# Attention scores of five batches over 64 rows, two heads side by side, in two bursts a batch

## The chip, the cores and the metric

The kernel runs on one core of one Trainium2 chip. The metric is the device time of one execution in microseconds (us); the span of an execution runs from its first to its last instruction and is a little shorter. The engines are called as in the profile: PE (TensorE, matmuls), PEld (its weight loads), ACT (ScalarE), DVE (VectorE), POOL (GpSimd) and SP (the queue that issues most DMAs). A matmul multiplies a stationary operand, loaded by LDWEIGHTS, with a moving operand that is streamed past it column by column; the result goes to a PSUM bank, of which there are eight.

## The reference

```python
def _attn_ref(q, k, v):                       # 8 batches, 8 heads, 576 positions, head size 64
    scores = np.matmul(q, k.transpose(0, 1, 3, 2)) / np.sqrt(64)
    rel = pos[:, None] - pos[None, :]
    mask_plain = (rel >= 0) & (rel < 32)                       # heads 0 to 3
    mask_dil = (rel >= 0) & (rel < 32 * 4) & (rel % 4 == 0)    # heads 4 to 7
    ... masked softmax over the keys, then attn @ v

def _moe_ref(x, w_tok1, w_tok2, w_ch1, w_ch2):   # x: 576 positions x 512 channels of a batch
    h = np.maximum(xt @ w_tok1, 0.0) @ w_tok2    # mixes tokens, 576 -> 256 -> 576
    u = x + h.transpose(0, 2, 1)
    h2 = np.maximum(u @ w_ch1, 0.0) @ w_ch2      # mixes channels, 512 -> 1536 -> 512
    return u + h2
```

The attention's output, heads side by side, is the `x` of the second part.

## The kernel before

The eight batches go through a software pipeline whose order is written out by hand. `gen_main(b)` is the main loop of batch b: the two channel matmuls, first `gp` (with its relus into `gt`, on ACT and DVE), then `yp` (evicted by DVE into `o`, stored by SP). It yields after every few matmuls an estimate of its own time, and `interleave` inserts the other batches' steps at given places on that clock: values, token mixing (`h1p`, `up`) of batch b+1 and casts, transposes and scores of batch b+2. So during main loops 1 to 5 the scores of batches 3 to 7 are computed. Odd batches' main loops also hold the 64-position tails of two batches (`gt` tiles of PSUM, `yp` first).

**Scores.** Heads go in pairs hp = 0..3; the first 64 partitions hold one head of the pair, the other 64 the second. `kt` holds k transposed in natural order, `kr` in order of remainder by 4. `qz[hp][:, h]` is q of head h with the other head's 64 rows set to zero, so one matmul over all 128 rows gives the scores of head h. Plain heads (hp 0, 1) need, for each head, blocks of 128 keys by 160 queries in a bank `sc`, and a small bank `sm` for the last block and the tail. Dilated heads (hp 2, 3) need four blocks of 128 by 128, one for each remainder, and a small bank. The exponential (ACT) goes to `attp` or `attd`; POOL multiplies by the band mask. Batches 0 to 2 hide scores in another way, with an added matmul of the identity and `veil`, or (batch 2) as the later ones.

**From batch 3 on** (`by_dma`), q and k are transposed by DMA into `qta` (`qt` in the profile), `kra` (`kr`) and `tta` (`tt`, the tails). `place_steps` then copies them: POOL writes `kt` and `qz` of the plain heads and the tails, DVE `qz` of the dilated heads and the last 128 keys of `kt`. `score_steps` gives the twelve places of a batch's score pieces; between two of them 6 or 12 matmuls of `yp` stand on PE.

**Banks.** `main` has three banks in turn (`gp`, `yp`), `sc` two (scores only, `sc` and `sm`), `fl` three (values `av`, `h1p`, `up`, transposes).

Of the kernel before, what the change touches and what calls it, by code (L numbers as in the profile page):

```python
# [16 lines left out]
S = 576  # L17
D = 64
WINDOW = 32
# [14 lines left out]
PTL = 4 * PST  # L34
PW = PTL + 192
DTL = 512
DW = DTL + 320
# [20 lines left out]
def _np_dtail():  # L58
    p = np.arange(128)[:, None]
    j = np.arange(64)[None, :]  # L60
    reach = WINDOW * DILATION
    out = []
    for k0 in (384, 512):
        rel = (512 + j) - (k0 + p)
        out.append((rel >= 0) & (rel < reach) & (rel % DILATION == 0))
    return np.stack(out, axis=1).astype(np.float16)
# [3 lines left out]
def kernel(  # L70
# [40 lines left out]
    def mult(eng, out, a, b):  # L111
# [4 lines left out]
    CW = 2 * 128 + BLK + 128  # L116
# [4 lines left out]
    dtail = const[:, 256 + BLK:CW].rearrange("p (x y c) -> p x y c", x=1, y=2)  # L121

    veil = fixed("veil", [128, BLK + 128])
# [4 lines left out]
         _np_dtail().reshape(128, 128)], axis=1)  # L128
# [29 lines left out]
    def emit_fixed():  # L158
# [5 lines left out]
        for a in attp:  # L164
            nc.gpsimd.memset(
                a[:, :, 0:PTL].rearrange("p h (b c) -> p h b c", c=PST)[:, :, :, BLK:PST], 0.0)
            nc.gpsimd.memset(a[:, :, PTL:PW], 1.0)
        for a in attd:
            nc.vector.memset(a[:, :, DTL:DW], 1.0)

# [190 lines left out]
    def place_steps(b):  # L361

        halves = [slice(0, 64), slice(64, 128)]

        def tails():
            eng = nc.vector if b == 3 else nc.gpsimd
            for h in range(2):
                eng.tensor_copy(out=qza[halves[h], :, h, 512:S], in_=tta[halves[h], :, 0:64])
            eng.tensor_copy(out=kta[:, :, 512:S], in_=tta[:, :, 64:128])

        def plain(hp):
            nc.gpsimd.tensor_copy(out=natural(kt[hp][:, 0:512]), in_=kra[:, hp].rearrange("p r m -> p m r"))
            for h in range(2):
                nc.gpsimd.tensor_copy(out=natural(qz[hp][halves[h], h, 0:512]),  # L374
                                      in_=qta[halves[h], hp].rearrange("p r m -> p m r"))

        def dil(h):
            nc.vector.tensor_copy(out=qza[halves[h], 2:4, h, 0:512],
                                  in_=qta[halves[h], 2:4].rearrange("p a r m -> p a (r m)"))

        def dil_k():
            for hp in (2, 3):
                nc.vector.tensor_copy(out=natural(kt[hp][:, 384:512]),
                                      in_=kra[:, hp, :, 96:128].rearrange("p r m -> p m r"))

        return ([tails] + [lambda hp=hp: plain(hp) for hp in range(2)],
                [lambda h=h: dil(h) for h in range(2)] + [dil_k])
# [27 lines left out]

    def scores_plain(b, hp):
        a = attp[hp]
        blocks = a[:, :, 0:PTL].rearrange("p h (b c) -> p h b c", c=PST)
        tl = a[:, :, PTL + 64:PTL + 128]
        veils = veiled(b, hp)  # L420
        wide, narrow = (veil[:, 0:BLK], veil[:, 0:64]) if veils else (None, None)
        for h in range(2):
            p = bank("sc", 2, f"sc_{b}_{hp}_{h}")
            for kb in range(3):
                score(b, hp, h, p[:, BLK * kb:BLK * kb + BLK], slice(128 * kb, 128 * kb + 128),
                      slice(128 * kb, 128 * kb + BLK), wide)
# [5 lines left out]
        for h in range(2):  # L432
            score(b, hp, h, p[:, BLK * h:BLK * h + BLK], slice(384, 512), slice(384, 384 + BLK), wide)
        for h in range(2):
            score(b, hp, h, p[:, 320 + 64 * h:384 + 64 * h], slice(512, 640), slice(512, S), narrow)
        nc.scalar.activation(  # L436
            out=blocks[:, :, 3, 0:BLK], in_=p[:, 0:320].rearrange("p (h c) -> p h c", c=BLK),
            func=AF.Exp, scale=0.125)
        nc.scalar.activation(
            out=tl, in_=p[:, 320:448].rearrange("p (h c) -> p h c", c=64), func=AF.Exp, scale=0.125)  # L440
        if not veils:
            mult(nc.gpsimd, blocks[:, :, :, 0:BLK], blocks[:, :, :, 0:BLK], band)
            mult(nc.gpsimd, tl, tl, band[:, 0, :, 0:64])
        yield 0.21

    def scores_dil(b, hp):
        a = attd[hp - 2]
        diag = a[:, :, 0:DTL].rearrange("p h (r c) -> p h r c", c=128)
        tl = a[:, :, DTL + 64:DTL + 320].rearrange("p h (x c) -> p h x c", c=128)[:, :, :, 0:64]
        veils = veiled(b, hp)  # L450
        for h in range(2):
            p = bank("sc", 2, f"sc_{b}_{hp}_{h}")
            for r in range(4):
                score(b, hp, h, p[:, 128 * r:128 * r + 128], kra[:, hp, r] if by_dma(b) else slice(r, 512, 4),
# [4 lines left out]
        for h in range(2):  # L459
            for x in range(2):  # L460
                score(b, hp, h, p[:, 128 * h + 64 * x:128 * h + 64 * x + 64],
                      slice(384 + 128 * x, 512 + 128 * x), slice(512, S),
                      veil[:, BLK + 64 * x:BLK + 64 * x + 64] if veils else None)
        nc.scalar.activation(
            out=tl, in_=p[:, 0:256].rearrange("p (h x c) -> p h x c", x=2, c=64),
            func=AF.Exp, scale=0.125)
        if not veils:
            mult(nc.gpsimd, diag, diag, band[:, :, :, 0:128])
            mult(nc.gpsimd, tl, tl, dtail)
        yield 0.12  # L470

    def values(b, h):
# [4 lines left out]
        if hp < 2:  # L477
# [7 lines left out]
            c0 = 3 * PST + (64 if odd else 128)  # L485
            c1 = PTL + (0 if odd else 64)
            nc.tensor.matmul(out=av[:, 4], lhsT=a[:, c0:c0 + 128], rhs=va[:, 3, h, :],
# [454 lines left out]
```

## Time and profile before

| | |
|---|---|
| median of 3 runs | 297.87 us (297.7 to 298.11) |
| the profiled execution | 297.69 us, span 295.8 us, granted clock 1.000 |
| PE | busy 280.8 us, 95% of the span |
| PEld | busy 218.7 us, 74% |
| POOL | busy 186.2 us, 63% |
| DVE | busy 156.9 us, 53% |
| ACT | busy 136.6 us, 46% |

A matmul's listed duration includes the way through the array, and consecutive matmuls overlap, so what a group of them costs PE is read from the distance between starts in the timeline, not from the durations. Main loop 1 starts at about 69.6 us of the span, loop 2 at 108.4, loop 3 at 138.1, loop 4 at 173.3, loop 5 at 203.1 and loop 6 at 238.

### The profile page before, as it was taken

The page shows a single profiled execution, that of the slowest core. Times are in us where ns is not written, and L with a number is a line of the kernel's source. Part 1 is how long each engine was busy: PE and PEld are TensorE (multiplying, and loading weights), DVE is VectorE, ACT ScalarE, POOL GpSimd, SP SyncE. Part 2 cuts the span into 40 slices and gives each one's busy share as a digit, 9 for nine tenths or more (in the row PEclk, how much of TensorE's full clock was granted, in tenths as well). Part 3 has the DMA queues.
Part 4 walks back from the last instruction along what each step waited for, and adds up shares of the span by engine and source line. Part 5 has one row for each costly group of instructions (what it writes and reads, how often), then busy time and mean ns, then how long its engine had stood idle before and what let it go on. Part 6 is the DMA issues. An engine that isn't in the chain of part 4 may idle for free.

```text
span 295.8 us, 7055 instructions
## 1 busy us (share of the span) xinstructions
PE 280.8 (95%) x2810; PEld 218.7 (74%) x2810; DVE 156.9 (53%) x303; ACT 136.6 (46%) x266; POOL 186.2 (63%) x256
## 2 busy tenths in 40 slices
PE   5698999988999999999999999999999999999994
PEld 2586589976776986698776976797777976896593
DVE  5766347855828637466743555486654364422022
ACT  3763336356663634556346715474355625224500
POOL 6982045538999899959976999679985920000000
PEclk9999999999999999999999999999999999999999
DMA  7999999999958978179987978399965220531032
GB/s 214 264 202 160 207 320 209 289 265 277 242 112 216 289 228 168 31 175 324 229 149 166 323 219 179 59 216 317 196 127 107 73 74 0 82 115 38 0 89 92
DMA packets 103473, 52.09 MB, mean 176 GB/s; under 512 B 71792, under 2 KB 102384, under 8 KB 103440
## 3 DMA queue, kind: packets, MB, share of 16 engines
q1 hardware_dynamic: 99200, 46.55, 63.8%
q0 software_dynamic: 2640, 3.91, 7.5%
q10 hardware_dynamic: 1600, 1.18, 1.3%
q8 instruction: 22, 0.36, 0.5%
q14 instruction: 11, 0.09, 0.1%
HBM read 37.04 MB, written 9.44 MB: 157 GB/s over the span
## 4 chain that ended last, share of the span: by engine, by line
PE 78%; DMA 10%; POOL 6%; issue 3%; ACT 2%; SPq 0%; DVE 0%; POOLq 0%; ACTq 0%
PE gp L646 26%; PE yp L665 25%; PE h1p L513 4%; PE up L525 4%; DMA w<-in_moe_w_ch_dram 4%; PE yp L685 4%; PE sc L407 3%; PE gt L637 3%; DMA l_k<-in_k_dram 2%; DMA l_vn<-in_v_dram 2%; DMA l_q<-in_q_dram 2%; POOL vv L103 1%; PE sm L407 1%; PE h1p L511 1%; PE av L483 1%
## 5 line engine op out<-in xcount | busy, mean ns | idle before, releaser
L665 PE MATMUL yp<-w,gt 128*128 128x256 f16 x756 | 92.2, 273 | 0.0
L107 ACT ACTIVATE gt<-gp 128x512 f16<-128x512 f32 x76 | 45.4, 597 | 78.5 <-PE gp L646 78.2
L665 PEld LDWEIGHTS <-gt 128*128 128x128 f16 x768 | 76.8, 106 | 5.2 <-issue 0.3
L646 PEld LDWEIGHTS <-w 128*128 128x128 f16 x384 | 40.0, 114 | 24.4 <-issue 2.0
L113 POOL TENSOR_TENSOR attp<-attp,const 128x1280 f16<-128x1280 f16 (+1 forms) x24 | 36.9, 1564 | 18.1 <-ACT attp L436 18.0
L646 PE MATMUL gp<-utd,w 128*128 128x512 f16 x120 | 45.6, 380 | 0.0
L646 PE MATMUL gp<-utm,w 128*128 128x512 f16 x120 | 45.5, 379 | 0.0
L675 DVE TENSOR_TENSOR o<-yp,u 128x512 f32<-128x512 f32 x31 | 21.2, 688 | 45.1 <-PE yp L665 42.5
L646 PE MATMUL gp<-uT,w 128*128 128x512 f16 x144 | 36.2, 379 | 1.5 <-DMA w<-in_moe_w_ch_dram 0.8
L113 POOL TENSOR_TENSOR attd<-attd,const 128x1024 f16<-128x1024 f16 (+1 forms) x24 | 32.8, 1398 | 0.0
L113 DVE TENSOR_TENSOR xn<-av,rec 128x320 f16<-128x320 f32 x64 | 31.5, 492 | 2.2
L407 PEld LDWEIGHTS <-kt 128*128 128x128 f16 x272 | 22.2, 101 | 5.1 <-issue 1.5
L427 ACT ACTIVATE attp<-sc 128x480 f16<-128x480 f32 x32 | 17.8, 572 | 9.8 <-PE sc L407 9.2
L531 DVE TENSOR_TENSOR u<-up,xn 128x512 f16<-128x512 f32 x26 | 18.0, 691 | 8.1 <-PE up L525 8.1
L374 POOL COPY qz<-qt 64x512 f16<-64x512 f16 x20 | 21.6, 1081 | 0.6
L103 POOL CAST c_q<-l_q 128x512 f16<-128x512 f32 x31 | 18.9, 615 | 4.4 <-DMA l_q<-in_q_dram 4.4
L109 DVE TENSOR_SCALAR gt<-gp 128x512 f16<-128x512 f32 x20 | 13.8, 688 | 12.4 <-PE gp L646 11.9
L103 POOL CAST c_k<-l_k 128x512 f16<-128x512 f32 x29 | 17.7, 613 | 2.8 <-DMA l_k<-in_k_dram 2.6
L456 ACT ACTIVATE attd<-sc 128x512 f16<-128x512 f32 x32 | 17.9, 600 | 2.7 <-PE sc L407 2.5
L407 PE MATMUL sc<-qz,kt 128*128 128x160 f16 (+1 forms) x144 | 18.1, 228 | 1.0 <-DVE kt L315 1.0
L107 ACT ACTIVATE h<-h1p 128x256 f16<-128x256 f32 x29 | 11.1, 383 | 16.5 <-PE h1p L513 16.4
L502 DVE RECIPROCAL rec<-av 128x5 f32<-128x5 f32 x64 | 12.1, 189 | 11.2 <-PE av L499 5.9
(139 smaller groups left out, 487.8 us busy)
## 6 DMA issues: line engine op xcount, KB each, us to landing
out_dram<-o SPq DMA_DIRECT2D x72, 128.0 KB, 3.0
l_q<-in_q_dram SPq DMA_DIRECT2D x15, 512.0 KB, 6.6
l_k<-in_k_dram SPq DMA_DIRECT2D x14, 512.0 KB, 7.0
l_vn<-in_v_dram SPq DMA_DIRECT2D x32, 128.0 KB, 5.6
l_vd<-in_v_dram SPq DMA_DIRECT2D x16, 256.0 KB, 3.8
w<-in_moe_w_ch_dram POOLq DMA_DIRECT2D x6, 512.0 KB, 8.6
lt<-in_q_dram SPq DMA_DIRECT2D x8, 128.0 KB, 4.0
l_vt<-in_v_dram SPq DMA_DIRECT2D x8, 128.0 KB, 3.7
```

What stands on the lines that cost most here:

```text
L103: eng.tensor_copy(out=out, in_=in_)
L107: nc.scalar.activation(out=out, in_=in_, func=AF.Relu)
L109: eng.tensor_scalar_max(out=out, in0=in_, scalar1=0.0)
L113: eng.tensor_tensor(out=out, in0=x, in1=y, op=ALU.mult)
L374: nc.gpsimd.tensor_copy(out=natural(qz[hp][halves[h], h, 0:512]), in_=qta[halves[h], hp].rearrange("p r m -> p m r"))
L407: nc.tensor.matmul(out=out, lhsT=lhsT, rhs=qz[hp][:, h, queries], start=hide is None, stop=True)
L427: nc.scalar.activation(out=blocks[:, h, 0:3, 0:BLK], in_=p[:, 0:3 * BLK].rearrange("p (b c) -> p b c", c=BLK), func=AF.Exp, scale=0.125)
L456: nc.scalar.activation(out=a[:, h, 0:DTL], in_=p, func=AF.Exp, scale=0.125)
L531: nc.vector.tensor_tensor(out=u16(b, s), in0=blocks4(p), in1=blocks4(xn[b][:, s]), op=ALU.add)
L646: nc.tensor.matmul(out=p, lhsT=w3_block(cb, mb), rhs=uT[(b, cb)][0], start=(i == 0), stop=(i == 3))
L665: nc.tensor.matmul(out=p[:, c], lhsT=gta[:, mb, a0:m0 + 512:4] if half else gta[:, mb, a0:a0 + 128], rhs=w4[mb][:, c], start=(mb == 0), st ...
L675: nc.vector.tensor_tensor(out=blocks4(o32), in0=blocks4(p), in1=u16(b, s), op=ALU.add)
```

## The change

For batches 3 to 7 the scores are computed by `scores_twin`, a burst for the plain heads (g = 0) and one for the dilated heads (g = 1). Each matmul takes the 64 rows of its own head: keys from the head's half of `kt` or `kr`, queries straight from `qt` and `tt`. The two heads of a pair alternate and write to different banks. A burst is 24 matmuls in a row and takes six banks: both of `sc`, all three of `fl`, one of `main`. Before, a batch's scores were 44 matmuls of 128 rows in twelve pieces; now they are 48 of 64 rows in two. Queries of the plain heads come out in the order of the remainder by 4, and the exponential reads PSUM with a stride so that it writes in order. The copies into `qz` are gone for these batches; the copies of the last keys move from DVE to POOL. The tails' weights go to a buffer of their own, `attt`, also for batches 0 to 2, whose small bank now holds 128 columns and two tail blocks of 64 for a head (before 160 and one). The first burst is placed behind the relus of `gp`.

On PE, in main loop 2 (scores of batch 4; `sc_0_0` is the bank of the first head of the pair 0, `sc_0_1` that of the second). Before, where the first piece stands between matmuls of `yp`:

```order
L665 MATMUL yp_0_2213<-w_85,gt 128x256
L407 LDWEIGHTS kt
L407 MATMUL sc_0_0_2228<-qz,kt 128x160
L407 LDWEIGHTS kt
L407 MATMUL sc_0_0_2228<-qz,kt 128x160
L407 LDWEIGHTS kt
L407 MATMUL sc_0_0_2228<-qz,kt 128x160
L665 LDWEIGHTS gt
L665 MATMUL yp_0_2213<-w_85,gt 128x256
```

After, the first rows of the burst in the same place:

```order
L736 MATMUL yp_0_2220<-w_85,gt 128x256
L476 LDWEIGHTS kt
L476 MATMUL sc_0_0_2228<-qt,kt 128x160
L476 LDWEIGHTS kt
L476 MATMUL sc_0_1_2229<-qt,kt 128x160
L476 LDWEIGHTS kt
L476 MATMUL sc_0_0_2228<-qt,kt 128x160
L476 LDWEIGHTS kt
L476 MATMUL sc_0_1_2229<-qt,kt 128x160
```

Three matmuls of one head became the first of 24 in which the heads alternate; behind the burst 30 matmuls of `yp` follow (26 in odd loops) before the second burst.

On ACT, in the same main loop (the exponentials, and the copies `utd` that the next main loop's `gp` reads). Before:

```order
L427 ACTIVATE attp_74<-sc_1_1_2294 128x3x160
L436 ACTIVATE attp_74<-sm_1_2316 128x2x160
L439 ACTIVATE attp_74<-sm_1_2316 128x2x64
L583 COPY utd<-utm_88 128x512
L456 ACTIVATE attd_75<-sc_2_0_2326 128x512
L456 ACTIVATE attd_75<-sc_2_1_2345 128x512
L464 ACTIVATE attd_75<-sm_2_2364 128x2x2x64
L583 COPY utd<-utm_88 128x512
L456 ACTIVATE attd_76<-sc_3_0_2374 128x512
```

After:

```order
L500 ACTIVATE attp<-sc_0_5_2233 128x2x128
L500 ACTIVATE attt<-sc_0_5_2233 128x2x2x64
L500 ACTIVATE attd_74<-sc_1_0_2314 128x512
L500 ACTIVATE attd_74<-sc_1_1_2315 128x512
L500 ACTIVATE attd_75<-sc_1_2_2316 128x512
L500 ACTIVATE attd_75<-sc_1_3_2317 128x512
L500 ACTIVATE attt<-sc_1_4_2318 128x2x2x64
L500 ACTIVATE attt<-sc_1_5_2319 128x2x2x64
L649 COPY utd<-utm_88 128x512 x2
```

The two copies `utd` stood among the dilated heads' exponentials; now both stand behind them.

On POOL, between the casts of batch 4 and its masks. Before:

```order
L368 COPY qz<-tt 64x4x64 x2
L369 COPY kt<-tt 128x4x64
L372 COPY kt<-kr 128x512
L374 COPY qz<-qt 64x512 x2
L372 COPY kt<-kr 128x512
L374 COPY qz<-qt 64x512 x2
L113 TENSOR_TENSOR attp_73<-attp_73,const 128x2x4x160
```

After:

```order
L367 COPY kt<-kr 128x512
L364 COPY kt<-tt 128x4x64
L367 COPY kt<-kr 128x512
L370 COPY kt<-kr 128x128 x2
L112 TENSOR_TENSOR attp<-attp,const 128x8x160
```

Six copies into `qz` left POOL, and two short ones of `kt` came from DVE.

```diff
-    attp = [fixed(f"attp{i}", [128, 2, PW]) for i in range(2)]
-    attd = [fixed(f"attd{i}", [128, 2, DW]) for i in range(2)]
+    attpa = fixed("attp", [128, 2, 2, PW])
+    attp = [attpa[:, i] for i in range(2)]
+    attd = [fixed(f"attd{i}", [128, 2, DTL]) for i in range(2)]
+    attt = fixed("attt", [128, 4, 2, TW])
...
-        for a in attd:
-            nc.vector.memset(a[:, :, DTL:DW], 1.0)
+        nc.vector.memset(attt, 1.0)
...
         def tails():
-            eng = nc.vector if b == 3 else nc.gpsimd
-            for h in range(2):
-                eng.tensor_copy(out=qza[halves[h], :, h, 512:S], in_=tta[halves[h], :, 0:64])
-            eng.tensor_copy(out=kta[:, :, 512:S], in_=tta[:, :, 64:128])
+            nc.gpsimd.tensor_copy(out=kta[:, :, 512:S], in_=tta[:, :, 64:128])
...
-    def scores_plain(b, hp):
...
+    def tail_scores(b, hp, p, c0):
+        for h in range(2):
+            for x in range(2):
+                c = c0 + 128 * h + 64 * x
+                v0 = BLK + 128 * (hp // 2) + 64 * x
+                score(b, hp, h, p[:, c:c + 64], slice(384 + 128 * x, 512 + 128 * x), slice(512, S),
+                      veil[:, v0:v0 + 64] if veiled(b, hp) else None)
...
+    def scores_twin(b, g):
+
+        tags = (("sc", 2), ("sc", 2), ("fl", 3), ("fl", 3), ("fl", 3), ("main", 3))
+        ps = [bank(*tags[i], f"sc_{b}_{g}_{i}") for i in range(6)]
+        small = ps[4:6]
+
+        def twin(hp, banks, c, keys, queries):
+            for h in range(2):
+                rows = slice(64 * h, 64 * h + 64)
+                n = c.stop - c.start
+                nc.tensor.matmul(out=banks[h][:, c], lhsT=keys(rows), rhs=queries(rows), start=True, stop=True)
+
+        for j in range(2):
+            hp = 2 * g + j
+            if g == 0:
+                for kb in range(3):
+                    twin(hp, ps[2 * j:2 * j + 2], slice(BLK * kb, BLK * kb + BLK),
+                         lambda rows: kt[hp][rows, 128 * kb:128 * kb + 128],
+                         lambda rows: qta[rows, hp, :, 32 * kb:32 * kb + 40])
+            else:
+                for r in range(4):
+                    twin(hp, ps[2 * j:2 * j + 2], slice(128 * r, 128 * r + 128),
+                         lambda rows: kra[rows, hp, r], lambda rows: qta[rows, hp, r])
+        for j in range(2):
+            hp = 2 * g + j
+            if g == 0:
+                twin(hp, small, slice(256 + 128 * j, 384 + 128 * j),
+                     lambda rows: kt[hp][rows, 384:512], lambda rows: qta[rows, hp, :, 96:128])
+            for x in range(2):
+                twin(hp, small, slice(128 * j + 64 * x, 128 * j + 64 * x + 64),
+                     lambda rows: kt[hp][rows, 384 + 128 * x:512 + 128 * x], lambda rows: tta[rows, hp, 0:64])
+        yield 0.87
+
+        def main(hp):
+            for h in range(2):
+                p = ps[2 * (hp % 2) + h]
+                if g == 0:
+                    exp(plain_blocks(hp)[:, h, 0:3, 0:BLK].rearrange("p b (m r) -> p b m r", r=4),
+                        p[:, 0:3 * BLK].rearrange("p (b r m) -> p b m r", r=4, m=40))
+                else:
+                    exp(attd[hp - 2][:, h], p)
...
     def score_steps(b, t0, dt, offs=(0.0, 0.7, 2.0), places=None):
 
         steps = []
+        if by_dma(b):
+            for g in range(2):
+                for i, f in enumerate([scores_twin(b, g)] * 2):
+                    steps.append((t0 + g * dt, 0.86 * (i == 0), lambda f=f: next(f)))
+            return steps
...
-            steps += score_steps(3, 22.2, 2.8) + at(9.0, 0.6, cast_steps(3))
+            steps += score_steps(3, 25.2, 4.2) + at(9.0, 0.6, cast_steps(3))
...
-                steps += at(2.0, 0.6, cast_steps(b + 2)) + score_steps(b + 2, 15.0 + late, 2.6)
-                steps += at(8.5, 0.7, dma_steps(b + 2)) + at(13.0, 0.4, place_steps(b + 2)[0])
+                steps += at(2.0, 0.6, cast_steps(b + 2)) + score_steps(b + 2, 16.6 + 1.25 * late, 4.5)
+                steps += at(8.5, 0.7, dma_steps(b + 2)) + at(12.0, 0.4, place_steps(b + 2))
```

More of the change, by code (lines that the diff above doesn't have):

```diff
@@ L33 @@
 PST = 256
-PTL = 4 * PST
-PW = PTL + 192
+PW = 4 * PST
 DTL = 512
-DW = DTL + 320
+TW = 320
 CBS = (2, 0, 3, 1)
@@ L458, in scores_dil @@
         p = small_bank(b, hp)
[L459 to L466, printed above, removed]
+        tail_scores(b, hp, p, 0)
```

129 lines of the change are left out of this document (74 added, 55 removed).

## The prediction

> **What bounds the kernel now.** I read the page's engine shares first, then the chain that ended last, then busy time by stretch, the list of PE's waits, and last the timeline around the scores.
>
> ```profile
> PE 280.8 (95%) x2810; PEld 218.7 (74%) x2810; DVE 156.9 (53%) x303; ACT 136.6 (46%) x266; POOL 186.2 (63%) x256
> PE 78%; DMA 10%; POOL 6%; issue 3%; ACT 2%; SPq 0%; DVE 0%; POOLq 0%; ACTq 0%
> 108.38:238.00 129.62, 128.74 (x1263) 100.20 (x1262) 72.97 (x128) 64.81 (x124) 111.65 (x138) 1.00 0.76 179
> 238.00:291.60 53.60, 53.60 (x451) 40.25 (x449) 18.68 (x36) 16.70 (x28) 0.48 (x1) 1.00 0.23 60
> PE sc L407 <- ACT attd L456: 0.3, 2, 0.2
> ```
>
> In the stretches the columns after the length are busy PE, PEld, DVE, ACT, POOL, then clock, DMA share and GB/s. From main loop 2 on PE lacks 0.9 us of 129.6, and nothing of the last 53.6; POOL is at 86% there but PE hardly waits for it. So a microsecond less in PE's stream is a microsecond less in the end, if PE then finds no new wait. The clock is full. What a score piece costs PE is the distance from its start to the next row's:
>
> ```profile
> 95.29 0.39 PE L550 MATMUL tpu<-const,u 128*128 128x128 f16 x4
> 95.51 0.37 PE L407 MATMUL sc<-qz,kt 128*128 128x160 f16 x3
> 95.72 0.82 PE L665 MATMUL yp<-w,gt 128*128 128x256 f16 x6
> 96.38 0.37 PE L407 MATMUL sc<-qz,kt 128*128 128x160 f16 x3
> 97.24 0.36 PE L407 MATMUL sm<-qz,kt 128*128 128x160 f16 x4
> 97.44 0.82 PE L665 MATMUL yp<-w,gt 128*128 128x256 f16 x6
> 103.12 0.28 PE L407 MATMUL sm<-qz,kt 128*128 128x64 f16 x4
> 103.23 0.82 PE L665 MATMUL yp<-w,gt 128*128 128x256 f16 x6
> 103.89 0.39 PE L407 MATMUL sc<-qz,kr 128*128 128x128 f16 x4
> 104.11 0.82 PE L665 MATMUL yp<-w,gt 128*128 128x256 f16 x6
> ```
>
> Three matmuls of 160 columns take 0.21 us (0.070 each), four of 128 take 0.22 (0.055), four of 64 take 0.11 (0.0275), the plain small bank 0.20, six of `yp` 0.66 (0.11): time goes by columns, and zero rows cost as much as others.
>
> **The change, part by part.** Removed from PE: four plain pieces and two small banks, 4 x 0.21 + 2 x 0.20 = 1.24 us, and four dilated pieces and two small banks, 4 x 0.22 + 2 x 0.11 = 1.10. That is 2.34 us a batch, 11.7 us for five.
>
> Added: burst 1 has 6 pairs of 160 columns, 2 of 128 and 4 of 64; burst 2 has 8 of 128 and 4 of 64. No row of before shows two half-height matmuls together, so I bound a pair. Low end: its heads stream side by side, and a pair costs what one full matmul of its columns does: 6 x 0.070 + 2 x 0.055 + 4 x 0.0275 = 0.64, and 8 x 0.055 + 4 x 0.0275 = 0.55, together 1.19 us. High end: one after the other, 2.38 us. The heads use different partitions, weights and banks, so nothing that the rows show is shared but the order of issue. I take the low end, with the 64-column pairs put at up to 0.055, since 0.0275 for one is the shortest distance in these rows and may be an issue limit: 1.19 to 1.41, taken as 1.30. Saved: 5 x (2.34 - 1.30) = 5.2 us; the ends are 5.75 saved and 0.2 lost.
>
> The edges. Each burst goes from full height to half height and back: 2 bursts x 2 x 5 batches = 20 edges. What an edge may cost is read from one matmul's own times:
>
> ```profile
> L407 PE MATMUL sc<-qz,kt x144: 217/232/245, 8.0 to 227.1; 128*128 128x160 f16 x96, 128*128 128x128 f16 x48
> L407 PEld LDWEIGHTS <-kt x272: 95/98/117, 8.0 to 233.7; 128*128 128x128 f16 x136
> ```
>
> A 160-column matmul lasts 232 ns from start to end and holds the next back for 70: 162 ns are its way out. A weight load lasts 98 ns and is hidden now, for starts are closer than that. If PE must be empty at an edge, the edge costs 0.16 us; if the load can't run ahead either, 0.26; if neither, 0. The nearest row for 0 is the change of kind from transposes to scores at 95.51, which costs nothing (0.22 for four, as within scores), but it does not change the array's division. I take the way out alone, 0.16, because loads are hidden everywhere in these rows: 20 x 0.16 = 3.2 us, ends 0 and 5.2. The Trainium skill bears on this: "TensorEngine Tiling (Array Packing)", section Tiling Modes, states that a change of the tiling mode, not of the tile alone, drains the TensorE. No run here shows it yet; by the row of 95.51 the sum below would be 292.5, by that rule it stays at 295.7.
>
> A stall that goes. In even loops the dilated exponentials stood behind a copy `utd`:
>
> ```profile
> 133.86 0.28 PE L407 MATMUL sm<-qz,kt 128*128 128x64 f16 x4
> 134.29 0.38 PE L407 MATMUL sc<-qz,kr 128*128 128x128 f16 x4 [0.15 <-ACT attd L456]
> 132.16 1.09 ACT L583 COPY utd<-utm 128x512 f16<-128x512 f16 x1
> 133.14 1.10 ACT L456 ACTIVATE attd<-sc 128x512 f16<-128x512 f32 x2
> ```
>
> 0.11 us after 133.86 the array is free, the next piece starts at 134.29: 0.32 us lost, in two loops by PE's waits (x2): 0.64 us gained. Late next there are the copies themselves, now both behind burst 2's exponentials. Two exponentials take 1.10, so 0.55 each. Burst 2 starts 0.69 + 30 x 0.11 + 0.32 (two edges) = 4.3 us after burst 1; its first bank is readable some 0.4 us later, four exponentials take 2.2, two small ones 0.8, and the two copies of 1.09 end at 9.9; the next main loop starts at 0.69 + 0.61 + 90 x 0.11 + 0.64 = 11.8. Covered by 1.9 us.
>
> Banks between the bursts. Burst 2 reuses burst 1's banks, so ACT must have read them.
>
> ```profile
> L427 ACT ACTIVATE attp<-sc 128x480 f16<-128x480 f32 x32 | 17.8, 572 | 9.8 <-PE sc L407 9.2 <-POOL qz L374 0.5
> L464 ACT ACTIVATE attd<-sm 128x256 f16<-128x256 f32 x16 | 6.1, 384 | 3.2 <-PE sm L407 3.2
> L583 ACT COPY utd<-utm 128x512 f16<-128x512 f16 x10 | 10.8, 1086 | 4.1 <-DMA utm<-u 4.1
> L101 ACT COPY uT<-tpu 128x512 f16<-128x512 f16 x3 | 1.8, 585 | 2.9 <-PE tpu L559 2.9
> L101 ACT CAST w1n<-w_p 128x512 f16<-128x512 f32 x2 | 1.2, 585 | 1.6 <-PE w_p L783 1.6
> ```
>
> The plain exponentials now read with a stride of 40 fp32 values. `uT` on ACT reads PSUM in that way (all of ACT's `uT` are the reordered ones) and lasts 585 ns, the straight cast `w1n` also 585; `utd`, strided from SBUF, 1086. A strided read of PSUM is nearest to `uT`, so I keep 572. Then the eight exponentials of burst 1 (four at 0.55, four at 0.384) end 0.4 + 2.2 + 1.5 = 4.1 us after its start, and burst 2 needs their last bank at 4.3 + 0.44: no wait. The high end, 1086, is a rival.
>
> New waits for `fl`. In main loop 1 burst 1 stands directly behind the last transposes, which use `fl`:
>
> ```profile
> 95.49 0.58 ACT L101 COPY uT<-tpu 128x512 f16<-128x512 f16 x1 [1.59 <-PE tpu L559]
> 96.38 0.41 DVE L103 COPY uT<-tpu 128x512 f16<-128x512 f16 x1
> ```
>
> PE wants the bank at 95.51 + 0.21 = 95.72 and gets it at 96.07: 0.35 us, once. The last of them, read by DVE until 96.79, would make it 0.9 at most, but DVE loses the `qz` and `kt` copies ahead of it. In later loops `fl` was left long before.
>
> Small bank of batches 1 and 2: 2 x 0.055 + 4 x 0.0275 = 0.22 for 0.195, for two pairs, and twice that in batch 1 with its `veil` matmuls: 0.15 us. Batch 0's 0.1 us and the start-up lie under PE's waits there:
>
> ```profile
> 10.61 0.40 PE L393 MATMUL tp_t<-const,c_t 128*128 128x128 f16 x4 [1.24 <-POOL c_t L103]
> 29.19 10.31 PE L646 MATMUL gp<-uT,w 128*128 128x512 f16 x47 [0.80 <-DMA w<-in_moe_w_ch_dram]
> 3.60 1.27 DVE L169 MEMSET attd<- 128x640 f16 x2
> L374 POOL COPY qz<-qt 64x512 f16<-64x512 f16 x20 | 21.6, 1081 | 0.6
> L383 DVE COPY kt<-kr 128x128 f16<-128x128 f16 x10 | 13.6, 1404 | 0.1
> 126.26 0.37 PE L407 MATMUL sc<-qz,kt 128*128 128x160 f16 x3
> 123.78 2.21 POOL L374 COPY qz<-qt 64x512 f16<-64x512 f16 x2
> 129.02 6.26 POOL L113 TENSOR_TENSOR attp<-attp,const 128x1280 f16<-128x1280 f16 x4 [3.04 <-ACT attp L436]
> ```
>
> The new memset has twice the elements of the two at 3.60, so DVE is 1.3 us later there, and the constants' DMA is a quarter larger; PE's 1.24 us of waiting for POOL at 10.61 cover it. I set 0; the ends are 0 and 0.3.
>
> POOL loses 4 x 1.08 us a batch, DVE the 1.4 us copies, which move to POOL two a batch. Both count 0: POOL already waited 3.04 us for ACT before the masks, and PE for neither. In loop 2 the last copy ended at 123.78 + 2.21 = 126.0; without four of 1.08 it is 121.7, for a burst that stands one `yp` group (0.66) ahead of 126.26. SP issues the same transposes in the same order.
>
> **Sum** against the profiled execution: 297.69 - 5.2 + 3.2 - 0.64 + 0.35 + 0.15 = 295.55. It stood 0.18 below the median of the runs, so the median would be 295.7, or 2.1 us (0.7%) less.
>
> **The rivals.**
> - Dear edges: the load after an edge is not hidden either, 0.26 each. For it: nothing can be loaded ahead into an array that is to be divided anew. Against: all loads in the rows run ahead. 295.7 + 2.0 = 297.7, no change.
> - Cheap edges, 0.03 each: 295.7 - 2.6 = 293.1. For it, the gapless change at 95.51.
> - The change doesn't do what it says: the heads of a pair run one after the other. The bursts cost 2.38 us instead of 1.30, so 295.7 + 5 x 1.08 = 301.1, slower. It decides from 1.7 us a batch for the two bursts on, where the edges eat what is saved. For it, that PE takes its matmuls in order and no row shows two at once; against, that the heads share no rows, weights or bank.
> - Loads not hidden at half height: each head waits for its own load and columns, so a pair costs 98 + 70 = 168, 153 or 126 ns: 6 x 0.168 + 2 x 0.153 + 4 x 0.126 + 8 x 0.153 + 4 x 0.126 = 3.55 us a batch, and 295.7 + 5 x 2.25 = 306.9. The Trainium skill's "TensorE: Matmul & The Clock Gate", section Part 3, says that a load overlaps matmuls in flight only where its row group differs, and here every second load has the same. The rows of now contradict it at full height: 98 ns loads stand under starts 70 ns apart, all on the same rows. So its chance is small.
> - Strided exponentials as slow as `utd`: 0.4 + 4 x 1.09 + 2 x 0.73 + 2 x 0.384 = 7.0 us against 4.74, so PE waits 2.25 us in each batch for the last bank: 295.7 + 11.2 = 306.9.
>
> **How the numbers follow.** Chances: my forecast 0.47 (its own range 294.2 to 297.2, by edges of 0.09 to 0.23), dear edges 0.22, cheap edges 0.12, one after the other 0.11, loads not hidden 0.04, slow exponentials 0.04. Ends of the range: cheap edges without any limit for the 64-column pairs (0.5 less) at the low side, 292.6; dear edges with the whole 0.9 us of the bank wait and 0.3 at the start at the high side, 298.6. The last three cases, 0.19, stay out. The least that a measurement of this kernel can tell from no change is about 0.2%, 0.6 us. Faster: 0.42 of my case, 0.12 of the cheap edges and 0.03 of the dear ones, 0.57. Same: 0.04 and 0.12, 0.16. Slower: 0.01, 0.07, and the last three, 0.27.
>
> **What would show it.** In the timeline of after: pairs of `sc` matmuls starting together, or 0.070 us apart for both; the distance from the last `yp` before a burst to the burst's first matmul, less 0.11, is an edge, likewise behind it. The whole burst 1, from that `yp` to the next, should take about 1.0 us, burst 2 0.9. ACT's plain exponentials should stay at 570 to 600 ns. PE's waits should hold no row of bursts against ACT, but for one of about 0.35 us near 95.7. The `utd` copies should end before `gp`. I would be wrong if bursts take 1.4 us or more each, or if the next `gp` or `av` waits for ACT or POOL.

## The result and the profile after

The changed kernel takes 294.38 us (median of 5 runs, 293.95 to 295.36); the kernel before, run beside it, 297.87 us (296.65 to 298.11). The ratio is 0.9896, 95% interval 0.9869 to 0.9923: 3.5 us or 1.0% faster. The profiled execution took 293.95 us with a span of 292.2 us, against 297.69 and 295.8.

The engine shares, the chain that ended last by engine, and the stretch from main loop 2 to about main loop 6 of the changed kernel (columns as in the prediction):

```profile
PE 278.1 (95%) x2850; PEld 213.4 (73%) x2850; DVE 133.2 (46%) x279; ACT 134.3 (46%) x266; POOL 166.3 (57%) x227
PE 84%; DMA 6%; POOL 5%; ACT 1%; SPq 1%; DVE 1%; issue 1%; POOLq 0%
...
108.49:235.13 126.64, 126.06 (x1284) 96.00 (x1283) 53.70 (x113) 62.92 (x124) 94.79 (x114) 1.00 0.80 185
```

PE is still the bound: it lacks 0.6 us of 126.6 (0.9 of 129.6 before). POOL fell from 186.2 to 166.3 us and DVE from 156.9 to 133.2; as neither was waited for, that by itself bought nothing. The gain is in PE's own stream. Main loop 2, timeline of PE in the changed kernel, from the first output matmul to the next loop's first channel matmul:

```profile
125.05 0.82 PE L736 MATMUL yp<-w,gt 128*128 128x256 f16 x6
125.81 0.65 PE L476 MATMUL sc<-qt,kt 64*128 64x160 f16 x14
126.29 0.22 PE L476 MATMUL sc<-tt,kt 64*128 64x64 f16 x4
126.34 0.22 PE L476 MATMUL sc<-qt,kt 64*128 64x128 f16 x2
126.40 0.22 PE L476 MATMUL sc<-tt,kt 64*128 64x64 f16 x4
126.55 3.45 PE L736 MATMUL yp<-w,gt 128*128 128x256 f16 x30
129.94 0.62 PE L476 MATMUL sc<-qt,kr 64*128 64x128 f16 x16
130.39 0.28 PE L476 MATMUL sc<-tt,kt 64*128 64x64 f16 x8
130.60 6.74 PE L736 MATMUL yp<-w,gt 128*128 128x256 f16 x60
137.18 0.38 PE L717 MATMUL gp<-utd,w 128*128 128x512 f16 x1
```

Read the starts. Fourteen score matmuls (six pairs of 160 columns, one of 128) fill 125.81 to 126.29: 0.48 us, which is 6 x 0.070 + 0.055, the time of seven full-height matmuls. Four of 64 columns take 0.05: two pairs at 0.0275. So both heads of a pair go in the time of one, down to 64 columns. The edges: six output matmuls from 125.05 are through at 125.71 (0.11 each), the burst begins at 125.81, 0.10 later; its own 0.64 us end at 126.45, the next output matmul starts at 126.55, again 0.10. Burst 2 shows 0.09 and 0.11.

The weight loads (PEld) around the burst's start, here and in the run at full height that is described below:

```profile
125.80 0.25 PEld L476 LDWEIGHTS <-kt 64*128 64x128 f16 x8 [0.21 <-issue]
```

```profile
126.55 0.41 PEld L476 LDWEIGHTS <-kt 128*128 128x128 f16 x5
```

At full height the burst's first load starts 0.11 us before its first matmul (126.66). In the changed kernel it starts together with the first matmul (125.81): at an edge no load runs ahead.

ACT in the same place, the two spots that stalled ahead of main loop 2, on PE, and ACT's copy that ends the second of these stalls:

```profile
126.28 2.23 ACT L500 ACTIVATE attp<-sc 128x480 f16<-128x480 f32 x5 [0.43 <-PE sc L476]
128.36 0.43 ACT L500 ACTIVATE attt<-sc 128x256 f16<-128x256 f32 x1
128.89 0.45 ACT L500 ACTIVATE attt<-sc 128x256 f16<-128x256 f32 x1
130.43 2.06 ACT L500 ACTIVATE attd<-sc 128x512 f16<-128x512 f32 x4 [1.08 <-PE sc L476]
132.88 2.13 ACT L649 COPY utd<-utm 128x512 f16<-128x512 f16 x2
...
79.99 0.29 PE L560 MATMUL av<-vv,attd 128*128 128x65 f16 x4
80.61 0.20 PE L563 MATMUL av<-vt,attt 128*128 128x65 f16 x1 [0.33 <-POOL attt L112]
...
95.83 0.39 PE L616 MATMUL tpu<-const,u 128*128 128x128 f16 x4
96.15 0.97 PE L476 MATMUL sc<-qt,kt 64*128 64x160 f16 x14
96.94 0.23 PE L476 MATMUL sc<-tt,kt 64*128 64x64 f16 x4
97.22 3.45 PE L736 MATMUL yp<-w,gt 128*128 128x256 f16 x30
...
96.03 0.59 ACT L100 COPY uT<-tpu 128x512 f16<-128x512 f16 x1 [1.59 <-PE tpu L625]
```

The kernel before, at the place of the row at 80.61:

```profile
79.73 0.28 PE L494 MATMUL av<-vv,attd 128*128 128x65 f16 x4
80.07 0.20 PE L497 MATMUL av<-vt,attd 128*128 128x65 f16 x1
```

Burst 1's exponentials end at 129.3, before burst 2 starts; ACT then waits for PE, not the other way round. The copies `utd` end at 135.0, 2.2 us ahead of the matmul that reads them. In main loop 1 burst 1 takes 1.07 us (96.15 to 97.22) where loop 2's takes 0.74: 0.33 us of waiting for a transpose bank, which ACT's copy `uT` frees at 96.62. At 80.61 batch 2's values of a dilated head wait for POOL's mask of their tail weights. The kernel before waited there too, but less: four of these matmuls take 0.12 us, the next one comes 0.34 us after the first (79.73 to 80.07) and now 0.62 us after it (79.99 to 80.61), so 0.28 us more are lost.

### The profile page after: what moved, and what is told of

Its sections match the earlier page's. It is cut to its first block, busy times and chain, and to the rows that moved or that the text cites. A ratio compares the mean times of both kernels' runs of the same rounds, so it can differ in the third digit from the quotient of the medians.

```text
span 292.2 us, 7087 instructions
## 1 busy us (share of the span) xinstructions
PE 278.1 (95%) x2850; PEld 213.4 (73%) x2850; DVE 133.2 (46%) x279; ACT 134.3 (46%) x266; POOL 166.3 (57%) x227
## 4 chain that ended last, share of the span: by engine, by line
PE 84%; DMA 6%; POOL 5%; ACT 1%; SPq 1%; DVE 1%; issue 1%; POOLq 0%
PE yp L736 28%; PE gp L717 27%; PE h1p L579 5%; PE yp L756 4%; PE up L591 4%; PE gt L708 3%; DMA l_q<-in_q_dram 3%; DMA w1p<-in_moe_w_tok_dram 2%; PE sc L476 2%; PE h1p L577 1%; PE av L560 1%; PE up L602 1%; POOL vv L102 1%; PE av L555 1%; POOL attp L112 1%; DMA l_vd<-in_v_dram 1%
## 5 line engine op out<-in xcount | busy, mean ns | idle before, releaser
L736 PE MATMUL yp<-w,gt 128*128 128x256 f16 x756 | 86.9, 273 | 0.0
L736 PEld LDWEIGHTS <-gt 128*128 128x128 f16 x768 | 78.4, 106 | 6.5 <-issue 0.3
L112 POOL TENSOR_TENSOR attp<-attp,const 128x1280 f16<-128x1280 f16 x12 | 31.3, 2611 | 33.7 <-ACT attp L500 27.5
L112 POOL TENSOR_TENSOR attd<-attd,const 128x1024 f16<-128x1024 f16 x12 | 25.3, 2123 | 0.0
L102 POOL CAST c_q<-l_q 128x512 f16<-128x512 f32 x31 | 19.7, 638 | 4.2 <-DMA l_q<-in_q_dram 4.2
L367 POOL COPY kt<-kr 128x512 f16<-128x512 f16 x10 | 10.8, 1078 | 7.9 <-DMA kr<-c_k 5.4
L500 ACT ACTIVATE attp<-sc 128x480 f16<-128x480 f32 (+1 forms) x30 | 13.4, 526 | 2.1 <-PE sc L476 2.1
L112 POOL TENSOR_TENSOR attt<-attt,const 128x512 f16<-128x512 f16 (+1 forms) x14 | 14.2, 1015 | 0.0
L393 PEld LDWEIGHTS <-kt 128*128 128x128 f16 x144 | 11.8, 103 | 3.2 <-issue 1.6
L606 DVE TENSOR_TENSOR u16t<-up,xn 64x512 f16<-64x512 f32 x7 | 4.8, 690 | 19.8 <-PE up L602 19.8
```

Of the source, the lines that this page charges most:

```text
L102: eng.tensor_copy(out=out, in_=in_)
L112: eng.tensor_tensor(out=out, in0=x, in1=y, op=ALU.mult)
L393: nc.tensor.matmul(out=out, lhsT=lhsT, rhs=qz[hp][:, h, queries], start=hide is None, stop=True)
L500: nc.scalar.activation(out=out, in_=in_, func=AF.Exp, scale=0.125)
L736: nc.tensor.matmul(out=p[:, c], lhsT=gta[:, mb, a0:m0 + 512:4] if half else gta[:, mb, a0:a0 + 128], rhs=w4[mb][:, c], start=(mb == 0), st ...
```

## The experiments

Two numbers stand beside each run's time. One is the ratio to the kernel before, measured on the same chip. The other is the stretch from main loop 2's first channel matmul to the end of the span, both read from the trace. It holds the scores of batches 4 to 7 and leaves out the start-up, which differs by up to 0.9 us between profiled executions with the same instructions up to there (107.55 for the bursts earlier, 108.49 for the changed kernel). The first lines give the changed kernel twice.

| kernel | median us | ratio to before (95%) | loop 2 starts | span | loop 2 to end |
|---|---|---|---|---|---|
| before | 297.87 | 1 | 108.38 | 295.8 | 187.42 |
| changed | 294.38 | 0.9896 (0.9869 to 0.9923) | 108.49 | 292.2 | 183.71 |
| changed, second measurement | 293.80 | 0.9885 (0.9844 to 0.9926) | 108.51 | 292.2 | 183.69 |
| heads apart | 298.48 | 1.0053 (1.0033 to 1.0072) | 108.69 | 296.2 | 187.51 |
| four bursts | 295.63 | 0.9948 (0.9927 to 0.9969) | 108.57 | 294.0 | 185.43 |
| full height | 297.67 | 1.0022 (1.0007 to 1.0037) | 109.44 | 296.2 | 186.76 |
| banks' order | 301.16 | 1.0121 (1.0098 to 1.0145) | 109.81 | 299.2 | 189.39 |
| bursts earlier | 301.19 | 1.0131 (1.0104 to 1.0158) | 107.55 | 298.4 | 190.85 |
| last keys on VectorE | 293.87 | 0.9883 (0.9860 to 0.9907) | 108.55 | 292.5 | 183.95 |
| both waits, mask on VectorE | 308.51 | 1.0387 (1.0362 to 1.0412) | | 306.1 | |
| two steps later | 292.93 | 0.9846 (0.9823 to 0.9868) | 107.08 | 290.7 | 183.62 |
| two steps later, again | 293.45 | 0.9882 (0.9847 to 0.9918) | 107.23 | 290.9 | 183.67 |

**Heads apart.** The heads of a burst no longer alternate.

```diff
+        todo = [[], []]
...
-                n = c.stop - c.start
-                nc.tensor.matmul(out=banks[h][:, c], lhsT=keys(rows), rhs=queries(rows), start=True, stop=True)
+                todo[h].append((banks[h][:, c], keys(rows), queries(rows)))
...
+        for o, k, q in todo[0] + todo[1]:
+            nc.tensor.matmul(out=o, lhsT=k, rhs=q, start=True, stop=True)
```

> The 24 matmuls of each burst stand head after head (12 of head 0, then 12 of head 1) and no longer alternate; everything else, the mode changes at a burst's ends included, is as in the changed kernel (294.4 us). Side by side: if a burst is short because two neighbouring matmuls in different halves run at the same time (0.070 us for a pair of 160 columns in its trace), the two bursts of a batch take 2.38 us of their own instead of 1.19, so 5 x 1.19 = +5.9 us: 300.3 us, with the 160-column matmuls 0.067 to 0.070 us apart. Rival, height: if matmuls of 64 rows are cheap by themselves, the order doesn't matter: 294.4 us. Rival, bare loads: if the load of the next weights is hidden only while the other half multiplies, 48 loads of some 0.075 us (213.4 us of loads over 2850) come bare on top of 2.38 us: 6.0 us for a batch's bursts, +24 us: 318 us.

Measured: 298.48 us, and 187.51 - 183.71 = 3.80 us more over four batches, 0.95 each. PE's timeline in main loop 2 of this run:

```profile
125.26 0.82 PE L739 MATMUL yp<-w,gt 128*128 128x256 f16 x6
126.01 0.64 PE L499 MATMUL sc<-qt,kt 64*128 64x160 f16 x7
126.50 0.22 PE L499 MATMUL sc<-tt,kt 64*128 64x64 f16 x2
126.53 0.24 PE L499 MATMUL sc<-qt,kt 64*128 64x160 f16 x2
126.61 0.19 PE L499 MATMUL sc<-tt,kt 64*128 64x64 f16 x1
...
127.28 3.45 PE L739 MATMUL yp<-w,gt 128*128 128x256 f16 x30
...
131.25 0.49 PE L499 MATMUL sc<-qt,kr 64*128 64x128 f16 x6
131.58 0.28 PE L499 MATMUL sc<-tt,kt 64*128 64x64 f16 x4
131.79 6.74 PE L739 MATMUL yp<-w,gt 128*128 128x256 f16 x60
```

Burst 1 takes 1.27 us (126.01 to 127.28) instead of 0.74. The height rival, which expected no change, falls: it is the neighbourhood of two matmuls in different halves that makes the burst short. The bare-loads rival (318 us) falls too: six matmuls of 128 columns in the same half start 0.055 us apart, four of 64 columns 0.0275. The side-by-side theory stands, but its 300.3 us were 1.8 too high. Part of that is at the seam: head 1's first matmul starts at 126.53, ahead of head 0's matmul at 126.61 that stands before it in the program. The bursts thus take 2.17 us a batch (126.01 to 127.28 and 130.66 to 131.79, less two edges of 0.11 behind them) and not 2.38, 1.0 us in five batches. The rest need not belong to the bursts: beside this run the kernel before, too, took 0.7 us less than beside the changed kernel (297.16 against 297.87).

**Four bursts.** Each burst is cut in two around output matmuls.

```diff
+            if j:
+                yield 0.4
+                ps += [bank(*tags[i], f"sc_{b}_{g}_{i}") for i in range(2, 6)]
...
-                for i, f in enumerate([scores_twin(b, g)] * 2):
-                    steps.append((t0 + g * dt, 0.86 * (i == 0), lambda f=f: next(f)))
+                for i, f in enumerate([scores_twin(b, g)] * 3):
+                    steps.append((t0 + g * dt + (0.0 if i == 0 else 1.35), (0.33, 0.53, 0.0)[i], lambda f=f: next(f)))
```

> Each burst is cut in two, with 6 or 12 full-height matmuls (output or channel matmuls of the main loop) between the halves: 40 changes of height instead of 20, same matmuls. Edges cost 0.10 us (changed kernel's trace: 0.10 us from the expected end of the last full-height matmul to the burst's first): +20 x 0.10 = +2.0 us, 296.4 us. Rival, no edge: the 0.10 us is the ordinary gap behind a six-matmul piece and no price of the height: 294.4 us. Rival, the edge as predicted (0.16 us, with part of it hidden in the bursts' own time): +3.2 us, 297.6 us. The exponentials come 1.3 us later; they have about 2 us to spare ahead of the next channel relus, so no wait is expected from that.

Measured: 185.43 - 183.71 = 1.72 us for 16 more edges, 0.107 each; by the ratios 0.52% or 1.5 us for 20, 0.08 each. PE's timeline in main loop 2:

```profile
125.14 0.82 PE L739 MATMUL yp<-w,gt 128*128 128x256 f16 x6
125.89 0.38 PE L475 MATMUL sc<-qt,kt 64*128 64x160 f16 x6
126.20 0.83 PE L739 MATMUL yp<-w,gt 128*128 128x256 f16 x6
126.97 0.44 PE L475 MATMUL sc<-qt,kt 64*128 64x160 f16 x8
```

Three pairs of 160 columns own 0.21 us and hold PE 0.31 (125.89 to 126.20); six output matmuls own 0.66 and hold it 0.77. The no-edge rival falls and so does 0.16 an edge, which would have given 297.6.

**Full height.** The bursts keep their places, with all 128 rows in each matmul.

```diff
-                nc.tensor.matmul(out=banks[h][:, c], lhsT=keys(rows), rhs=queries(rows), start=True, stop=True)
+                nc.tensor.matmul(out=banks[h][:, c], lhsT=keys(slice(0, 128)), rhs=queries(slice(0, 128)), start=True, stop=True)
```

> The bursts stay where they are, with the same count and order of matmuls, but each matmul takes all 128 rows of keys and queries (so it adds up both heads' scores; the separation of the heads is left out). No side by side and no change of height. Theory (pairs 1.19 us, edges 0.10 us): +5 x 1.19 for matmuls one after the other, -20 x 0.10 for the edges: 294.4 + 5.95 - 2.0 = 298.3 us, with no gap of 0.10 us at a burst's ends. Rival, edges belong to any burst (first weights or operands from other tiles): the gaps stay: 300.3 us. Rival, the gain came from gathering the scores in two bursts behind the relus and from the copies that went, not from half height: 294.4 to 295 us.

Measured: 297.67 us, and 186.76 - 183.71 = 3.05 us for four batches, 0.76 each; expected were 1.19 - 0.40 = 0.79. PE's timeline in main loop 2:

```profile
126.01 0.82 PE L736 MATMUL yp<-w,gt 128*128 128x256 f16 x6
126.66 1.10 PE L476 MATMUL sc<-qt,kt 128*128 128x160 f16 x14
...
127.95 3.44 PE L736 MATMUL yp<-w,gt 128*128 128x256 f16 x30
131.22 1.06 PE L476 MATMUL sc<-qt,kr 128*128 128x128 f16 x16
...
132.35 6.72 PE L736 MATMUL yp<-w,gt 128*128 128x256 f16 x60
```

The six output matmuls end into the burst without a gap (126.01 + 0.65 = 126.66), so the 0.10 us belongs to the change of height and not to a burst as such. The bursts take 1.29 + 1.13 = 2.42 us. This kernel has the gathered bursts, the place behind the relus and none of the copies `qz`, and it is as slow as the kernel before (ratio 1.0022). From main loop 2 on it is 0.66 us shorter than before (the stall behind `utd` is gone), but main loop 2 starts 1.1 us later. So without half height the rest of the change is worth nothing. The heads alternate between banks here as in the changed kernel, so it isn't the change of banks that makes a pair cheap.

**Banks' order.** The plain exponentials read their bank straight and write in steps.

```diff
-                    exp(plain_blocks(hp)[:, h, 0:3, 0:BLK].rearrange("p b (m r) -> p b m r", r=4),
-                        p[:, 0:3 * BLK].rearrange("p (b r m) -> p b m r", r=4, m=40))
+                    exp(plain_blocks(hp)[:, h, 0:3, 0:BLK].rearrange("p b (m r) -> p b r m", r=4),
+                        p[:, 0:3 * BLK].rearrange("p (b r m) -> p b r m", r=4, m=40))
...
```

> The plain exponentials walk in the order of the bank again: they read PSUM straight on and write the weights in steps of four elements, instead of reading PSUM in steps and writing straight on. Nothing else changes (294.4 us). Theory (a step on the SBUF side of ScalarE is what is dear, as the copies utd show with 1.06 us for 512 columns against 0.585 us for a straight activation): the four plain main exponentials of a batch go from 0.55 to about 1.0 us, the two small ones from 0.43 to 0.6, some +2.1 us of ScalarE a batch; burst 2 comes 4.1 us after burst 1 and then finds its banks held some 1 to 2 us: +5 to +10 us in all, 299 to 304 us. Rival (writing in steps is as cheap as reading PSUM in steps): 294.4 us, exponentials 0.55 us as now.

Measured: 301.16 us. The group of ACT (behind the first bar: busy us, mean ns) and the first of PE's waits in this run, and behind them the group in the changed kernel:

```profile
L500 ACT ACTIVATE attp<-sc 128x480 f16<-128x480 f32 x20 | 22.3, 1316 | 2.1 <-PE sc L476 2.1
PE sc L476 <- ACT attt L500: 2.6, 6, 0.6
```

```profile
L500 ACT ACTIVATE attp<-sc 128x480 f16<-128x480 f32 x20 | 9.8, 575 | 2.1 <-PE sc L476 2.1
```

The same exponentials take 1316 ns when they write in steps of four fp16 elements, 575 when they read PSUM in steps and write straight. The cost was larger than expected (1.0 us) and the mechanism as expected: burst 2 waits for burst 1's banks. So the walk in the order of the output is a condition of the gain.

**Bursts earlier.** Batches 4 to 7, both bursts 2.0 earlier in the plan.

```diff
-                steps += at(2.0, 0.6, cast_steps(b + 2)) + score_steps(b + 2, 16.6 + 1.25 * late, 4.5)
+                steps += at(2.0, 0.6, cast_steps(b + 2)) + score_steps(b + 2, 14.6 + 1.25 * late, 4.5)
```

> Batches 4 to 7: both bursts are planned 2.0 earlier (14.6 instead of 16.6), so that the first stands ahead of the last six or so channel matmuls and its exponentials ahead of the last channel relus on ScalarE. Theory (the place behind the relus matters): the exponentials of a burst take about 3.6 us of ScalarE; the last channel relu waits behind them, and the output matmuls need it 2.5 to 3.5 us after the burst: a wait of about 1.5 us in each of four batches, +6 us: 300.4 us, shown as output or channel matmuls that wait for ScalarE. Rival (ScalarE has room, 46% busy): within 0.5 us of 294.4.

Measured: 301.19 us, and 190.85 - 183.71 = 7.1 us in four batches, 1.8 each (expected 1.5). PE's waits of this run (total us, times, longest):

```profile
PE yp L756 <- ACT gt L106: 3.7, 2, 1.8
...
PE up L591 <- ACT attp L500: 1.5, 2, 0.8
```

In odd loops the output matmuls wait 1.8 us for the last channel relu, which stands behind the exponentials; in even loops the mixing waits 0.8 us for a bank that the burst took from the `fl` ring. These rows make 5.2 of the 7.1 us; smaller ones (0.5 us of bursts waiting for an eviction, 0.3 us of output matmuls waiting for a relu) come on top. ACT's 46% of busy time did not mean that it had room there.

**Last keys on VectorE.** One part undone: the copies of the last keys go back to VectorE.

```diff
         def dil(hp):
-            nc.gpsimd.tensor_copy(out=natural(kt[hp][:, 384:512]),
+            nc.vector.tensor_copy(out=natural(kt[hp][:, 384:512]),
```

> One part of the change undone: the copies of the last keys of the dilated pairs (128x128, two a batch) go back from GpSimd to VectorE. Theory (a VectorE instruction that takes both operands from SBUF is held until GpSimd has a gap): the copy stands in VectorE's queue while GpSimd runs its casts and copies back to back (111.1 to 122.8 us in the changed kernel's trace of main loop 2), so it holds VectorE for 1.4 us (its mean before) to 4 us, the evictions of the mixing behind it are late, and TensorE waits 0.5 to 1.5 us a batch: +2 to +7 us, 296.5 to 301 us. Rival (VectorE is 46% busy and hides it; GpSimd's queue is 0.75 us shorter): 294.4 us or a little less.

Measured: 293.87 us, ratio 0.9883: no change, the rival holds. Ten copies in this run (min/median/max ns), and the same ten in the kernel before:

```profile
L370 DVE COPY kt<-kr x10: 252/264/857, 93.4 to 220.1; 128x128 f16<-128x128 f16 x10
```

```profile
L383 DVE COPY kt<-kr x10: 379/876/2698, 99.8 to 229.7; 128x128 f16<-128x128 f16 x10
```

My picture of the place was wrong: with the `qz` copies gone, POOL's queue is at its last copy or empty by the time VectorE reaches these copies, so most take their own 0.26 us. Where POOL was still at work they were held, but only to the end of that one POOL instruction: the copy of 857 ns ends at 94.30, 0.13 us after POOL's copy beside it (94.17). The copies reached PE once: in main loop 4 burst 1 lost 0.29 us to an eviction behind them, which accounts for the 0.24 us by which the stretch is longer. In the kernel before it was alike, with longer POOL instructions: the copy of 2698 ns starts at 132.29, beside a mask that ends at 134.85, and ends at 134.99, although POOL has no pause there (its four masks, from 129.02 on, stand in the prediction as one row) and runs the next one from 134.82 to 135.28.

**Both waits, mask on VectorE.** Batch 3's burst later, and batch 2's dilated tail masks on VectorE instead of GpSimd.

```diff
-            mult(nc.gpsimd, tail_cols(hp), tail_cols(hp), tails_seen[1])
+            mult(nc.vector if b == 2 else nc.gpsimd, tail_cols(hp), tail_cols(hp), tails_seen[1])
...
-            steps += score_steps(3, 25.2, 4.2) + at(9.0, 0.6, cast_steps(3))
+            steps += score_steps(3, 26.0, 4.2) + at(9.0, 0.6, cast_steps(3))
```

> Two waits that the change brought are taken away: batch 3's first burst is planned 0.8 later (26.0 instead of 25.2), behind the copies that free the transposes' banks, and the tail masks of batch 2's dilated pairs go to VectorE, so that batch 2's values don't wait 0.33 us for GpSimd's. If both waits are on the path: -0.33 - 0.33 = 293.7 us. Rival: the burst's wait moves (the second burst or the later output matmuls wait instead) and VectorE's mask delays an eviction: 294.4 us, or up to 294.9.

Measured: 308.51 us, 14 us slower than the changed kernel, which no theory had. This run's timelines of VectorE and of GpSimd, and the first of PE's waits:

```profile
75.43 17.11 DVE L112 TENSOR_TENSOR attt<-attt,const 128x256 f16<-128x256 f16 x1
...
94.32 0.28 DVE L112 TENSOR_TENSOR attt<-attt,const 128x256 f16<-128x256 f16 x1
```

```profile
75.27 0.66 POOL L112 TENSOR_TENSOR attt<-attt,const 128x256 f16<-128x256 f16 x1
...
91.67 0.72 POOL L370 COPY kt<-kr 128x128 f16<-128x128 f16 x2
```

```profile
PE av L560 <- DVE xn L112: 14.2, 1, 14.2
```

The same mask takes 0.28 us at 94.32, when GpSimd is idle, and 17.11 us at 75.43. GpSimd runs without a pause from 75.27 to 92.39, through 27 instructions, and the mask ends at 92.54, 0.15 us after the last of them: unlike the copies of the experiment before, it did not get its turn behind one GpSimd instruction. Behind it stood the evictions for which PE waited 14.2 us.

**Two steps later.** The same two waits without that mask: the burst later, and the values of batch 2's first dilated head four channel matmuls later.

```diff
-            steps += late[10:] + va[:4] + [(9.6 + (0.0, 0.8, 2.8, 3.6)[i], c, f) for i, (_, c, f) in enumerate(va[4:])]
+            steps += late[10:] + va[:4] + [(9.6 + (0.7, 1.0, 2.8, 3.6)[i], c, f) for i, (_, c, f) in enumerate(va[4:])]
...
-            steps += score_steps(3, 25.2, 4.2) + at(9.0, 0.6, cast_steps(3))
+            steps += score_steps(3, 26.0, 4.2) + at(9.0, 0.6, cast_steps(3))
```

> The two small waits once more, without VectorE's mask, which in the run before was held 17 us until GpSimd's queue ran dry: batch 3's first burst is planned 0.8 later, and the values of batch 2's first dilated head stand four channel matmuls (0.86 us) later, behind GpSimd's mask. If both waits were on the path: -0.33 - 0.33 = 293.7 us. Rival: the next instruction waits instead (the burst for its main bank, the values of the next head): 294.4 us.

Measured: 292.93 us, ratio 0.9846 (0.9823 to 0.9868). Both waits are gone: the values run on without a gap, and burst 1 of main loop 1 takes 0.75 us (95.70 to 96.45). From a row of output matmuls in main loop 0, the same in both (46.43 us; 47.05 in the changed kernel), to the first channel matmul of main loop 3 (135.78; 137.18) it takes 89.35 us against 90.13: 0.78 us less. That is about what both waits cost by the starts, 0.33 us in the burst and 0.5 us (0.62 - 0.12) at 80.61. The other 0.6 us of its profiled execution come from an earlier start, ahead of both edits. So I ran both kernels once more, side by side on one chip.

> The changed kernel once more, unaltered, beside the version with the two later steps on the same chip. Expected from its first measurement: ratio to the kernel before 0.990, about 294.3 us.

> The version with batch 3's first burst and batch 2's first dilated values planned later, on the same chip as the changed kernel. If the two waits of 0.33 us are what it saves: 0.6 to 0.9 us less than the changed kernel beside it. Rival: its 1.4 us in the first measurement were mostly the start-up of that run (in its trace the first output matmuls of main loop 0 already stand 0.6 us earlier, ahead of both edits): no difference, within 0.3 us.

Measured: 293.80 us for the changed kernel and 293.45 for the later version. In the traces the stretch is again 0.78 us shorter (46.59 to 135.93 against 47.09 to 137.21), but the medians differ by 0.35 us and the intervals of the ratios overlap. The two waits are removed, and the version's median is the lower one both times (by 1.45 us in separate measurements, by 0.35 side by side); that the whole kernel is faster by the 0.78 us of the stretch is not settled by these runs.

## Why the prediction was right, point by point

Forecast 295.7, measured 294.38: the right sign, inside the forecast's own range, 1.3 us too high.

- **Pairs side by side: right, and better than put.** The two bursts own 1.19 us a batch, the low end; I had taken 1.30 for fear of an issue limit at 64 columns. None shows: a pair of 64 columns takes 0.0275 us. That term is off by 5 x 0.11 = 0.55 us. The rival "heads one after the other" was built as a run and gives 298.5, not the 301.1 that the prediction priced: 1.2 us of the difference are the edges, priced too dear, 1.0 us the overlap at the seam, and 0.4 us are not accounted for.
- **Edges: the mis-sized term.** I took a matmul's whole way out, 0.162 us, and got 3.2 us. Three runs give 0.10 to 0.12 (0.10 in the changed kernel's own gaps; 0.107 by sixteen more edges; 0.12 from the full-height run, (2.42 - 1.19 - 0.76) / 4): 20 x 0.10 = 2.0 us, 1.2 us less than predicted. The step that failed is "If PE must be empty at an edge, the edge costs 0.16 us". Its reason failed with it: loads are hidden inside the bursts and outside, but not at an edge, where the first load starts with its matmul. That was my condition for dear edges of 0.26 us, and the edge still costs 0.10. What fills the 0.10 us stays open: an array that empties in less than the recorded way out would fit, and so would one load (92 to 98 ns in the records) that is no longer hidden. No run here separates the two. The Trainium skill's "TensorEngine Tiling (Array Packing)", section Tiling Modes, says that a change of tiling mode drains the TensorE. The gaps fit that, at 0.10 us, and the full-height run shows that they go when the mode stays.
- **The stall behind `utd`: right.** The waits are gone, and the copies end 2.2 us ahead of their reader (1.9 predicted).
- **The bank wait in main loop 1: right**, 0.33 us for 0.35.
- **Exponentials: right.** 575 ns for the strided plain ones (572 predicted), no wait between bursts; the rival's mechanism is real if the step is put on the other side (1316 ns).
- **Loads not hidden inside a burst: wrong, as its small chance said.** The Trainium skill's "TensorE: Matmul & The Clock Gate", Part 3, lets a load run ahead only where its row group differs from the matmuls in flight. The trace disagrees: with the heads apart, all loads of a run hit the same half and last 92 to 95 ns in the records, and matmuls of 64 columns still start 0.0275 us apart.
- **Missed: the longer wait at 80.61 us**, 0.28 us more than before. I had counted the small bank's new columns on PE, but not on POOL. There the plain masks of one pair took 2.98 us from 67.96 before and take 3.24 from 67.99 now, and the dilated mask two pairs later starts at 77.81 instead of 77.27, with the values right behind it.
- **Small banks of batches 1 and 2: right**, 0.2 us for 0.15 (by the starts of one pair in each, 0.46 us instead of 0.39 in batch 1, 0.23 instead of 0.20 in batch 2).

With the measured sizes the sum closes within 0.2 us: 297.69 - 5 x 1.15 + 20 x 0.10 - 0.64 + 0.33 + 0.28 + 0.20 = 294.11, against 293.95 of the profiled execution. By stretches: until main loop 2 the change lost 0.1 us (108.38 to 108.49), and from there on it gained 3.71, of which 4 x (1.15 - 0.40) + 0.64 = 3.64 are explained.

## What to carry to other kernels

Where two products contract over 64 rows each, issue them in turn for the two halves of the array: they run in the time of one, but each entry into and exit from half height costs about 0.10 us here, so gather them until a burst saves clearly more than 0.2 us. Such a burst drops several banks of work on the engine that empties them: put it where nothing urgent stands behind on that engine, and let ScalarE's strided side be the PSUM read and not the SBUF write. Before a multiply of two SBUF operands is given to VectorE, look at how long GpSimd runs without a pause there, not at how busy VectorE is.

## What the runs showed of the hardware that I had not expected

- A VectorE multiply of two SBUF operands, 0.28 us by itself, took 17.11 us beside a GpSimd queue that never paused: it did not get its turn after one GpSimd instruction but after 27. The Trainium skill's "SBUF — State Buffer", section "Who interferes with whom", states that such an instruction contends with a GpSimd instruction that reads SBUF. This run agrees, and here the wait lasted until GpSimd's queue ran dry. VectorE's copies of the last keys waited for one GpSimd instruction only (they ended 0.13 us behind it, at 94.30 and at 134.99). Why the multiply was passed over and the copies were not, no run here shows.
- ScalarE: stepping through PSUM by 40 fp32 values is free (575 ns against 572 straight), stepping through SBUF on the write side by four fp16 values is not (1316 ns).
- With one head's matmuls ahead of the other's, the first of the second half starts before the last two of the first half (126.53 against 126.61 and 126.64), although it stands behind them in the program: between the halves the starts are not in program order.
